# Zero products behind the narrower product of a bank, and another order of the steps

## The chip, the core and the metric

The kernel runs on one NeuronCore of a Trainium2 chip. Five engines work side by side, each through its own instructions in program order: TensorE (PE in the profile; its weight loads are the row PEld), VectorE (DVE), ScalarE (ACT), GpSimd (POOL) and SyncE (SP). They wait for one another through semaphores. The metric is the device time of one execution in microseconds, lower is better. Before the change the median of three runs is 690.34 us (690.3 to 690.51).

## The reference

Four batches of cross-covariance attention are followed by a two-layer network with a tanh GELU:

```python
B, N, C = (4, 6080, 256)
qn = q / (np.linalg.norm(q, axis=1, keepdims=True) + 1e-06)
kn = k / (np.linalg.norm(k, axis=1, keepdims=True) + 1e-06)
s = kn.transpose(0, 2, 1) @ qn / tau          # 256 x 256 per batch
a = np.exp(s - s.max(-1, keepdims=True))
a /= a.sum(-1, keepdims=True) + 1e-09
x = (v @ a).reshape(B * N, C)                 # 24320 tokens of 256
h = x @ w_in                                  # 2048 wide
g = 0.5 * h * (1.0 + np.tanh(c * (h + 0.044715 * h * h * h)))
out = g @ w_out
```

Inputs and output are float32 in DRAM; the products are made in bfloat16.

## The kernel before, in words

**Stages.** The attention matrix of a batch and `w_in` are multiplied into one matrix `aw` (256 x 2048), so that a token block needs two products: `v` with `aw`, then GELU, then `w_out`. The tokens are cut into 25 blocks, numbered 0 to 24: five of 1024 and one of 960 tokens in each of the first three batches (so blocks 5, 11 and 17 have 960), and five of 1024, one of 512 (block 23) and one of 448 (block 24) in the last. A block is worked on in two halves of tokens; half a block is 512, 480, 256 or 224 columns. While one batch's blocks are worked on, the next batch's q and k are loaded and its Gram matrix, norms and `aw` are made.

**Two recursions.** Most of both products are made by a scheme with seven products in place of eight, whose sums are formed inside the accumulator banks.

- First layer, for block n and index i, steps `m1` to `m7` (`small`, L539): `m1` starts bank RB. `wcq` (L584, on ACT) copies RB into another bank, on which `m2` then accumulates; `m6` goes on in RB. `m5` starts a bank that `wy5` (ACT, L590) copies to a buffer. `wap` (DVE, L593) writes RB plus that buffer into a further bank, on which `m3` accumulates; `m7` goes on in RB; `wax` (DVE, L596) writes RB plus the buffer into `xw`; `m4` ends RB. `wGp`, `wGs`, `wGr`, `wGx` (ACT, L602 and L604) are the four GELUs. Some columns are made by plain products instead: `g` (`plain`, L493) and its GELU `G` (L510).
- Second layer, for block n and half h of the features: `T1` to `T4` (L671 on DVE; `T3` of blocks 1 to 22 is an accumulating DMA from POOL, L665) form sums of GELU outputs; `M1` to `M7` (`product`, L675) are the products, four matmuls a step; `cq` (ACT, L739), `y5` (ACT, L742), `ap` (DVE, L745) and `ax` (DVE, L748) play the parts of the `w` steps; `c11`, `c12`, `c21`, `c22` (DVE, L718) turn results for the stores (L731; SP, in the last blocks POOL and ACT too). Block 24 uses direct products `D` (`direct`, L698).

**Banks.** All accumulators share one pool of eight banks of 512 float32 columns, which the order names by the letters a to g and z. Any step that starts an accumulator says which bank it takes. Blocks of different widths use the same banks.

**Zeros.** `wcq`, `wap`, `cq` and `ap` let ACT or DVE write a sum into a bank on which matmuls then accumulate with `start=False`. The code wants every column of that sum to have been written by a matmul since the bank was last started. `BITS` holds, for each bank, how many columns that is. When the last product that started a bank was narrower than the new sum (480 columns before one of 512, say), `fill` (L484), called by `set_sum` (L566) and `next_sum` (L693), issues a matmul of zeros over the missing columns right where the new sum begins; the copying engine's write comes after it.

```python
def fill(acc, tag, w):
    x0 = BITS.get(tag, 0) // 32 * 32
    for x in range(x0, w, 256):
        mm(acc[:, x : min(w, x + 256)], lhsT=ones_bf, rhs=zeros_bf[:, 0 : min(w, x + 256) - x],
           start=x == 0, stop=True)
    BITS[tag] = max(w, BITS.get(tag, 0))
```

**The order.** After a prologue written as code (the first batch's Gram matrix, until about 38 us), the whole program is a string, `ORDER`, of 3,946 words, each a step such as `cq@b:10` (step `cq` of block 10 into bank b) or `m6.3:17` (step `m6`, index 3, block 17). They are issued one after another (`run`, L850), so the string sets the order on every engine's queue. `lq`, `lk` and `lv` issue the loads of q, k and v on POOL and wait for the last matmul issued before them; `lt` (L446) issues the transposing load of a half of v on SP; `vs` (DVE, L534 to L537) forms sums of v for `m4` to `m7`; `row` (L205) are Gram products; `qsq`, `ksq`, `f1` to `f3`, `sp`, `sa` are the norms; `aw` and `ac` (L375, L384, L386) make `aw`; the words that begin with `p` prepare the combined `w_out`.

Of the kernel before, what the change touches and what calls it, by code (L numbers as in the profile page):

```python
# [932 lines left out]
g.0_0@e:1 g.15_1@c:0 g.1_0@a:0 G.13_0:0 g.2_0@g:1 g.12_1@f:0 lv.1:1 G.1_0:0 g.7_0@d:0 g.2_1@a:0
G.0_0:1 pS4:0 G.2_0:1 g.10_1@e:0 G.12_1:0 ksq.0:1 qsq.0:1 row.0_5@z:1 g.10_0@g:0 G.7_0:0 lk.1:1
G.10_1:0 G.15_1:0 g.14_1@f:0 g.9_1@d:0 row.0_3:1 row.0_0:1 g.11_0@e:0 G.5_0:0 G.9_1:0 G.14_1:0
G.10_0:0 row.0_4:1 lt.1:1 G.2_1:0 g.13_1@c:0 T1.1:0 g.8_0@b:1 g.10_0@d:1 g.4_0@f:1 row.0_1:1 pNA:0
G.13_1:0 G.11_0:0 f1.0:1 T1.0:0 M1.1@g:0 lv.0:2 g.3_0@a:1 G.3_0:1 g.11_1@c:0 T3.1:0 f2.0:1 pA12:0
G.11_1:0 G.8_0:1 G.4_0:1 T2.0:0 f3.0:1 m1.1@e:1 M1.0:0 lq.2:1 row.0_2:1 M5.1@a:0 vs:1 g.0_1@c:1
row.1_3:1 row.1_2:1 wcq.1@b:1 G.0_1:1 G.10_0:1 row.1_5:1 row.1_4:1 lq.3:1 row.1_0:1 g.4_1@f:1 cq@c:0
G.4_1:1 row.1_1:1 M5.0:0 g.3_1@d:1 m5.1@f:1 m6.1:1 gc:1 G.3_1:1 wy5.1:1 y5:0 T2.1:0 lk.2:1 sp.0@z:1  # L940
M2.0:0 qsq.1:1 m2.1:1 g.12_0@d:1 M2.1:0 lv.1:2 T3.0:0 wap.1@f:1 c11:0 g.8_1@a:1 G.12_0:1 wGp.1:1
ksq.1:1 m7.1:1 m3.1:1 wax.1:1 g.10_1@d:1 f1.1:1 wGs.1:1 G.10_1:1 g.7_1@g:1 m5.5@b:1 G.8_1:1 T4.0:0
m1.6@f:1 lk.3:1 M6.0:0 m4.1:1 G.7_1:1 wy5.5:1 m1.5@d:1 wGr.1:1 sa.0:1 wcq.5@a:1 M6.1:0 g.2_1@g:1
f2.1:1 m2.5:1 ap@b:0 wcq.6@e:1 f3.1:1 m6.5:1 m6.6:1 m2.6:1 wGp.5:1 M7.0:0 M7.1:0 wap.5@a:1 lt.1:2
wGx.1:1 G.2_1:1 sp.1@z:1 g.12_1@g:1 T4.1:0 lt.0:2 M3.0:0 lq.4:1 wGp.6:1 qsq.2:1 m3.5:1 m7.5:1 M3.1:0
sa.1:1 ax:0 ksq.2:1 f1.2:1 M4.1:0 m5.6@e:1 wax.5:1 c12:0 lk.4:1 f2.2:1 M4.0:0 g.11_1@b:1 f3.2:1
sp.2@z:1 c21:0 wGs.5:1 G.12_1:1 sa.2:1 wGx.5:1 wy5.6:1 g.7_0@a:1 g.15_0@g:1 g.15_1@e:1 wap.6@c:1
ksq.3:1 row.2_1@z:1 m3.6:1 row.3_1:1 m4.5:1 qsq.3:1 G.15_1:1 wGs.6:1 G.11_1:1 f1.3:1 row.3_0:1
m7.6:1 row.3_3:1 G.7_0:1 row.3_5:1 row.2_0:1 wax.6:1 g.0_0@e:2 lk.5:1 T1.0:1 g.12_0@c:2 lq.5:1
T3.0:1 f2.3:1 row.3_4:1 wGr.5:1 m4.6:1 m1.3@b:2 G.0_0:2 m1.1@a:2 g.4_0@d:2 row.2_5:1 row.2_2:1  # L950
row.2_3:1 vs:2 G.12_0:2 wcq.3@e:2 m5.1@c:2 G.15_0:1 wGr.6:1 m6.3:2 m2.3:2 T1.1:1 wcq.1@g:2 wy5.1:2
m5.3@f:2 row.2_4:1 row.3_2:1 gc:1 f3.3:1 m6.1:2 g.11_0@c:1 m2.1:2 wy5.3:2 wGp.3:2 wGp.1:2 G.4_0:2
wGx.6:1 G.11_0:1 M5.1@f:1 wap.1@e:2 M5.0:1 wap.3@g:2 m5.5@d:2 T2.0:1 m3.3:2 m7.3:2 sp.3@z:1 y5:1
wGs.3:2 wax.3:2 lv.0:3 m7.1:2 g.8_1@c:2 M1.1@f:1 wGx.3:2 lk.6:1 m4.3:2 T3.1:1 T2.1:1 g.12_1@g:2
M1.0:1 qsq.4:1 ksq.4:1 m3.1:2 G.8_1:2 wax.1:2 g.4_1@c:2 wGr.3:2 G.12_1:2 cq@b:1 G.4_1:2 f1.4:1
m1.2@g:2 wGs.1:2 T4.0:1 wcq.2@c:2 f2.4:1 M2.0:1 M6.1:1 sa.3:1 m5.2@e:2 lv.1:3 f3.4:1 M2.1:1 m2.2:2
wy5.5:2 wy5.2:2 m1.5@d:2 m6.2:2 lq.6:1 wGp.2:2 m4.1:2 wcq.5@e:2 c11:1 wGr.1:2 wap.2@c:2 wGx.1:2
lt.1:3 M6.0:1 m2.5:2 lt.0:3 c22:0 ap@f:1 wGp.5:2 m7.2:2 wax.2:2 m3.2:2 g.0_1@a:2 sp.4@z:1 m6.5:2
M3.0:1 m4.2:2 wGs.2:2 qsq.5:1 ksq.5:1 sa.4:1 wap.5@e:2 G.0_1:2 f1.5:1 M3.1:1 wGr.2:2 wGx.2:2
m1.7@c:2 m7.5:2 m3.5:2 m1.6@a:2 wGs.5:2 g.8_0@g:2 c12:1 wcq.6@f:2 f2.5:1 G.8_0:2 M7.0:1 m5.6@e:2  # L960
wax.5:2 wcq.7@g:2 m2.6:2 m4.5:2 f3.5:1 M7.1:1 m2.7:2 m6.6:2 wy5.6:2 wGr.5:2 m5.7@e:2 sp.5@z:1 T4.1:1
m6.7:2 wGp.6:2 ax:1 M4.0:1 wap.6@d:2 sa.5:1 m7.6:2 wy5.7:2 wap.7@f:2 lq.7:1 wGx.5:2 wax.6:2 qsq.6:1
wGx.6:2 row.4_1@z:1 M4.1:1 m4.6:2 row.4_3:1 m7.7:2 m3.6:2 row.5_1:1 row.5_0:1 row.5_2:1 row.5_3:1
wGp.7:2 ksq.6:1 m1.2@e:3 c21:1 wax.7:2 m4.7:2 row.4_2:1 m3.7:2 wGs.6:2 wGr.6:2 wcq.2@b:3 f1.6:1
row.5_5:1 wGr.7:2 row.4_4:1 m1.1@g:3 m2.2:3 wGs.7:2 g.0_1@d:3 wGp.2:3 wcq.1@a:3 lk.7:1 vs:3 m5.1@c:3
row.4_0:1 T1.0:2 f2.6:1 g.0_0@f:3 m5.2@b:3 m6.1:3 row.5_4:1 m6.2:3 wy5.1:3 G.0_0:3 m2.1:3 T3.0:2
wap.1@c:3 wy5.2:3 G.0_1:3 M1.0@f:2 wGp.1:3 wGx.7:2 m3.1:3 g.8_1@b:3 m7.1:3 wGs.1:3 G.8_1:3 T1.1:2
M1.1:2 wap.2@d:3 wax.1:3 cq@a:2 lv.0:4 row.4_5:1 m3.2:3 m5.3@c:3 m4.1:3 M2.1:2 m1.3@b:3 wGx.1:3
lv.1:4 wy5.3:3 wGs.2:3 f3.6:1 gc:1 T2.1:2 wcq.3@c:3 wGr.1:3 T2.0:2 m7.2:3 sp.6@z:1 T3.1:2 M2.0:2
M5.0@d:2 wax.2:3 qsq.7:1 c11:2 m6.3:3 m2.3:3 m4.2:3 M6.1:2 wGp.3:3 wGr.2:3 wap.3@g:3 c22:1 m5.4@f:3  # L970
m1.4@c:3 T4.0:2 m7.3:3 M5.1:2 wGx.2:3 wcq.4@e:3 wy5.4:3 y5:2 m2.4:3 m3.3:3 m6.4:3 M6.0:2 wGs.3:3
wax.3:3 wap.4@f:3 ap@d:2 m5.5@g:3 wGp.4:3 wGx.3:3 m7.4:3 lt.1:4 m3.4:3 m4.3:3 wy5.5:3 lt.0:4
m1.5@e:3 M7.0:2 wcq.5@g:3 wax.4:3 sa.6:1 wGs.4:3 m6.5:3 m2.5:3 wGx.4:3 ksq.7:1 wap.5@f:3 m4.4:3
M7.1:2 m3.5:3 m7.5:3 f1.7:1 wGr.4:3 wGp.5:3 m1.6@c:3 wGr.3:3 m5.6@g:3 M3.0:2 ax:2 wcq.6@b:3 wax.5:3
m2.6:3 wy5.6:3 lv.0:5 wGs.5:3 wGp.6:3 m6.6:3 m4.5:3 wGr.5:3 g.8_0@g:3 m1.7@f:3 G.8_0:3 f2.7:1 M4.0:2
T4.1:2 wap.6@b:3 lk.0:2 wcq.7@e:3 m3.6:3 m5.7@g:3 f3.7:1 m7.6:3 sp.7@z:1 T1.0:3 m6.7:3 wGx.5:3
wax.6:3 wy5.7:3 sa.7:1 wGx.6:3 m2.7:3 wap.7@g:3 M3.1:2 M4.1:2 wGs.6:3 wGp.7:3 c12:2 lq.0:2 m7.7:3
m4.6:3 wax.7:3 m3.7:3 g.0_1@b:4 wGr.6:3 wGs.7:3 m4.7:3 c21:2 vs:4 m1.1@d:4 m1.2@e:4 G.0_1:4 T1.1:3
wcq.1@c:4 row.7_5@z:1 row.6_5:1 wGr.7:3 m5.1@g:4 row.7_4:1 lv.1:5 m2.1:4 row.7_0:1 m5.2@a:4
row.6_1:1 m6.1:4 pow:1 row.6_0:1 wcq.2@b:4 wy5.1:4 wGx.7:3 m2.2:4 wy5.2:4 wap.1@f:4 kf:1 T3.1:3  # L980
T3.0:3 wGp.1:4 wGp.2:4 m6.2:4 row.7_2:1 row.7_3:1 m7.1:4 m1.3@g:4 wcq.3@a:4 wax.1:4 row.7_1:1
row.6_2:1 m3.1:4 wGs.1:4 lq.1:2 row.6_4:1 wGx.1:4 wap.2@c:4 T2.0:3 g.0_0@b:4 m4.1:4 row.6_3:1
m5.3@f:4 G.0_0:4 wy5.3:4 m6.3:4 m7.2:4 m2.3:4 m3.2:4 gc:1 M1.1@b:3 m5.4@f:4 wax.2:4 T2.1:3 m4.2:4
wGr.1:4 wGs.2:4 m1.4@d:4 wGp.3:4 wap.3@c:4 ksq.0:2 wGr.2:4 M1.0:3 wcq.4@a:4 M5.1@e:3 m2.4:4 m7.3:4
kr:1 wGx.2:4 wy5.4:4 m3.3:4 m6.4:4 M5.0:3 c22:2 wax.3:4 m4.3:4 wap.4@f:4 krp@z:1 m3.4:4 T4.1:3
wGp.4:4 wGs.3:4 m7.4:4 cq@a:3 M2.0:3 wGx.3:4 lt.1:5 m5.5@c:4 wGs.4:4 S.1:1 S.0:1 m1.5@f:4 wax.4:4
# [319 lines left out]
```

## Time and profile before

| | |
|---|---|
| Median of three runs | 690.34 us (690.3 to 690.51) |
| Profiled execution | 690.15 us |
| Its span, from the first to the last instruction | 688.0 us |
| PE busy | 662.0 us, 3,517 instructions recorded |
| ACT busy | 621.9 us |
| DVE busy | 612.6 us |
| Granted TensorE clock over the span | 0.998 |

The span is the time between the first and the last instruction; 2.15 us of the profiled execution lie outside it. A row of the timeline gives the start in microseconds from the span's start, the time it took, the engine, the line, the operation with its output and inputs, and in brackets how long the engine was idle before it and what released it. The ends of matmuls are modelled: a matmul of 512 columns is shown as 0.38 us long although the next one starts 0.216 us later, so lost time on PE is read from start to start. A few matmul records are missing from the trace; such a hole is as long as one matmul.

### The profile page before, as it was taken

The numbers are of one execution on the slowest core, as the hardware profiler recorded it, in microseconds if no ns is written. First come the engines' busy times: TensorE is split into PE (matmuls) and PEld (weight loads), VectorE is DVE, ScalarE is ACT, GpSimd is POOL, SyncE is SP. The second block draws the span as 40 slices with busy tenths as digits, with TensorE's granted clock in tenths as the row PEclk, the third lists the DMA queues.
The fourth block names the chain that finished last, engine by engine and source line by source line (L and its number), as shares of the span: only waits on it lengthen the run. The fifth ranks groups of instructions, "written<-read, shape, count | busy, mean of one in ns | idle before, by whom it ended". The sixth has DMA issues, their size and how long they took to land.

```text
span 688.0 us, 10545 instructions
## 1 busy us (share of the span) xinstructions
PE 662.0 (96%) x3517; PEld 336.1 (49%) x3579; DVE 612.6 (89%) x941; ACT 621.9 (90%) x1193; POOL 115.0 (17%) x181
## 2 busy tenths in 40 slices
...
GB/s 240 208 251 138 150 180 162 167 189 120 184 129 159 183 186 120 171 95 162 162 114 174 162 149 179 136 154 148 81 114 116 119 134 124 131 94 155 94 87 92
DMA packets 167848, 101.70 MB, mean 148 GB/s; under 512 B 149217, under 2 KB 152929, under 8 KB 167073
## 3 DMA queue, kind: packets, MB, share of 16 engines
...
q8 instruction: 28, 0.46, 0.3%
...
## 4 chain that ended last, share of the span: by engine, by line
PE 87%; ACT 7%; DVE 2%; DMA 2%; issue 1%; SPq 0%; DVEq 0%; ACTq 0%
PE rb L481 17%; PE p L481 16%; PE q L481 13%; PE r L481 11%; PE m L481 10%; PE h L481 10%; PE G L205 6%; ACT g L602 3%; PE awp L375 2%; DMA qk_f<-in_q_dram 1%; ACT q L584 1%; PE o L481 1%; ACT yw L590 1%; PE warm L269 1%; PE ss L263 1%
## 5 line engine op out<-in xcount | busy, mean ns | idle before, releaser
L481 PEld LDWEIGHTS <-wcomb 128*128 128x128 bf16 x1408 | 136.7, 98 | 146.4 <-issue 4.5
L602 ACT ACTIVATE g<-q 128x512 bf16<-128x512 f32 (+1 forms) x286 | 170.8, 621 | 5.3 <-PE q L481 4.4
L481 PEld LDWEIGHTS <-aw 128*128 128x128 bf16 x807 | 78.1, 98 | 81.9 <-issue 4.6
L593 DVE TENSOR_TENSOR q<-rb,yw 128x512 f32<-128x512 f32 (+2 forms) x150 | 102.1, 686 | 13.6 <-PE rb L481 4.1
L671 DVE TENSOR_TENSOR t<-g,t 128x2048 bf16<-128x2048 bf16 (+2 forms) x96 | 112.8, 1180 | 1.0 <-ACT g L510 0.8
L596 DVE TENSOR_TENSOR xw<-rb,yw 128x512 f32<-128x512 f32 (+2 forms) x150 | 100.9, 675 | 12.3 <-PE rb L481 7.1
L481 PE MATMUL rb<-tv,sw 128*128 128x512 bf16 (+3 forms) x307 | 106.6, 367 | 1.4 <-DVE q L593 0.8
L510 ACT ACTIVATE g<-h 128x512 bf16<-128x512 f32 (+1 forms) x164 | 97.1, 654 | 4.1 <-PE h L481 4.0
L584 ACT ACTIVATE q<-rb 128x512 f32<-128x512 f32 (+2 forms) x150 | 91.4, 618 | 8.1 <-PE q L481 3.3
L590 ACT ACTIVATE yw<-m 128x512 f32<-128x512 f32 (+2 forms) x150 | 92.7, 621 | 6.2 <-PE m L481 3.7
L602 ACT ACTIVATE g<-xw 128x512 bf16<-128x512 f32 (+1 forms) x143 | 92.7, 650 | 3.3 <-DVE xw L596 3.1
L481 PE MATMUL r<-g,wcomb 128*128 128x512 bf16 (+2 forms) x377 | 94.2, 373 | 1.2 <-ACT p L739 0.7
L481 PE MATMUL p<-t,wcomb 128*128 128x512 bf16 (+2 forms) x372 | 93.3, 373 | 0.5
L481 PE MATMUL h<-vT,aw 128*128 128x512 bf16 (+2 forms) x321 | 90.3, 377 | 1.8 <-DVE aw L415 1.1
L481 PEld LDWEIGHTS <-sw 128*128 128x128 bf16 x628 | 61.1, 98 | 62.4 <-issue 3.2
L602 ACT ACTIVATE g<-rb 128x512 bf16<-128x512 f32 (+1 forms) x143 | 87.7, 618 | 1.3 <-PE rb L481 1.2
L665 POOL DMA_DIRECT2D g<-g x44 | 39.5, 933 | 180.3 <-ACT g L602 78.2
L671 DVE TENSOR_TENSOR t<-g 128x2048 bf16<-128x2048 bf16 (+2 forms) x48 | 56.7, 1182 | 0.1
L481 PE MATMUL m<-tv,sw 128*128 128x512 bf16 (+3 forms) x156 | 56.1, 367 | 0.4 <-ACT yw L590 0.2
L481 PE MATMUL rb<-tv,aw 128*128 128x512 bf16 (+3 forms) x157 | 55.7, 367 | 0.2
L481 PE MATMUL rb<-vT,aw 128*128 128x512 bf16 (+3 forms) x157 | 55.0, 367 | 0.3
L481 PE MATMUL q<-vT,aw 128*128 128x512 bf16 (+3 forms) x153 | 54.1, 367 | 1.2 <-ACT q L584 1.2
...
## 6 DMA issues: line engine op xcount, KB each, us to landing
...
```

Source lines behind the costliest of these rows:

```text
L205: nc.tensor.matmul(G[b][:, jc, :], lhsT=qt[:np_, r, jc * 128 : jc * 128 + 128], rhs=kt[:np_, r, :], start=first and jc == 0, stop=jc == 1, ...
L263: nc.tensor.matmul(SS[1], lhsT=ones_bf, rhs=sq[:, 256:512], start=c == 0 and r == 0, stop=end)
L375: nc.tensor.matmul(ps, lhsT=ET[b][:, jc, ic * 128 : ic * 128 + 128], rhs=win_bf[:, jc, fs * 512 : fs * 512 + 512], start=jc == 0, stop=jc ...
L481: GATE[0] = nc.tensor.matmul(*a, skip_group_check=True, **kw)
L510: nc.scalar.activation(g_half(n, u // 8)[:, x, u % 8], hp[:, :hc], AF.Gelu_apprx_tanh)
L584: nc.scalar.activation(Q[n, i, 0][:, :w], RB[n, i][:, :w], AF.Copy)
L590: nc.scalar.activation(YW[n, i][:, :w], M5.pop((n, i))[:, :w], AF.Copy)
L593: nc.vector.tensor_add(Q[n, i, 1][:, :w], RB[n, i][:, :w], YW[n, i][:, :w])
L596: nc.vector.tensor_add(XW[n, i][:, :w], RB[n, i][:, :w], YW.pop((n, i))[:, :w])
L602: nc.scalar.activation(g[:, t, k0], x[:, :w], AF.Gelu_apprx_tanh)
L665: nc.gpsimd.dma_start(out=o, in_=quarter(n, 1, 1, h), accum_op=ALU.add)
L671: (nc.vector.tensor_add if add else nc.vector.tensor_sub)(o, a, b)
```

## The change

Two things change. First, a new function `pads` walks through the order before the program is built and finds each product that starts a bank with fewer columns than the next sum in that bank needs. Behind that product, `begun` issues the matmul of zeros over the missing columns at once, and notes the full width in `BITS`, so that `fill` finds nothing to do where the sum begins. Second, the words of `ORDER` are put in another sequence: the same 3,946 steps, of which 3,807 stand at another place (13 places away on average) and 790 of those that name a bank name another one. With the order before, 8 sums call for zeros (`cq` and `ap` of blocks 4 and 10, `wcq.6` of block 12, `ap` of block 16, `wcq.2` of block 18, `wap.1` of block 24); with the order after, there are 9 narrower products with zeros behind them.

```diff
+    def pads():
+        last, res = {}, {}
+        for pos, word in enumerate(ORDER.split()):
+            what, _, n = word.partition(":")
+            what, _, tag = what.partition("@")
+            name = what.partition(".")[0]
+            if tag in ("", "z"):
+                continue
+            hc = hc_of(int(n)) if name != "aw" else 512
+            w = hc if name in ("M1", "M5", "cq", "ap") or hc > 256 else 2 * hc
+            if name in ("wcq", "wap", "cq", "ap"):
+                if tag in last and last[tag][1] < w:
+                    res[last[tag][0]] = max(w, res.get(last[tag][0], 0))
+            else:
+                last[tag] = (pos, w)
+        return res
+
+    PADS, STEP = pads(), [0]
+
+    def begun(acc, tag, w):
+
+        end = PADS.get(STEP[0], w)
+        if end > w:
+            mm(acc[:, w:end], lhsT=ones_bf, rhs=zeros_bf[:, 0 : end - w], start=False, stop=True)
+        BITS[tag] = max(w, end)
...
@@ plain
-        BITS[tag] = w = hc if wide else t
+        w = hc if wide else t
...
+        begun(hp, tag, w)
@@ small
-            BITS[tag] = U * hc
...
+        if m in (1, 5):
+            begun(acc, tag, U * hc)
@@ product
-            BITS[tag] = hc
...
+        if first:
+            begun(ACC[n, acc], tag, hc)
...
-        for word in ORDER.split():
+        for STEP[0], word in enumerate(ORDER.split()):
             run(word)
...
 ORDER = """
-g.2_0@f:0 g.3_0@g:0 g.0_0@a:0 aw.2@b:0 aw.3@c:0 ac.2:0 vp.1@z:0 ac.3:0 g.6_0@d:0 aw.5@e:0 G.2_0:0
-G.3_0:0 vc.1_0:0 G.6_0:0 G.0_0:0 vc.1_1:0 aw.4@f:0 g.4_0@g:0 aw.6@b:0 ac.5:0 aw.7@c:0 ac.4:0
...
-wap.3@g:11 aw.3@c:2 m4.2:11 wGs.2:11 m7.3:11 m3.3:11 cq@b:10 ac.3:2 M2.1:10 wGx.2:11 m1.5@c:11
...
-m3.5:11 aw.5@e:2 M2.0:10 ac.7:2 m1.6@g:11 wy5.7:11 ac.5:2 wGs.5:11 wax.5:11 ap@f:10 M3.0:10
...
-c12:23 wax.3:24 m3.3:24 D.5_0:24 wGr.2:24 D.2_1@e:24 m4.3:24 wGs.3:24 D.2_0:24 m2.3:24 wGx.1:24
-wGp.3:24 D.0_1:24 wGr.3:24 wGx.3:24 wGx.2:24 c22:23 D.4_1:24 D.1_1:24 D.3_0:24 D.5_1:24 D.6_0:24
-D.7_0:24 D.7_1:24 D.3_1:24 D.6_1:24 c11:24 c21:24 sB:24 c12:24 c22:24 sA:24
+g.3_0@f:0 g.0_0@g:0 g.2_0@a:0 aw.2@b:0 aw.3@c:0 ac.2:0 ac.3:0 g.1_0@d:0 vp.1@z:0 vc.1_1:0 vc.1_0:0
+g.7_0@e:0 aw.5@b:0 ac.5:0 G.7_0:0 aw.4@c:0 G.2_0:0 g.5_0@e:0 ac.4:0 aw.7@a:0 ac.7:0 lk.0:1 g.4_0@b:0
+G.1_0:0 G.0_0:0 G.5_0:0 G.3_0:0 g.3_1@d:0 G.3_1:0 g.10_1@g:0 g.2_1@c:0 aw.6@e:0 g.9_0@a:0 g.1_1@f:0
...
+m4.4:11 wy5.1:11 ac.4:2 wGs.4:11 m1.3@a:11 M5.1@f:10 m5.2@g:11 T1.0:10 wGr.4:11 ac.0:2 wGp.1:11
...
+m4.2:11 T2.0:10 wy5.5:11 m3.3:11 cq@g:10 m1.5@b:11 m7.3:11 wGx.2:11 M2.1:10 wax.3:11 M2.0:10
...
+m4.5:11 ap@a:10 M3.1:10 wy5.6:11 M7.1:10 wGx.5:11 wGr.5:11 ac.5:2 T4.1:10 wap.6@e:11 m7.6:11 c22:9
...
+D.5_0:24 m3.3:24 m3.2:24 D.5_1:24 m4.3:24 wGs.3:24 D.0_0:24 wGs.2:24 wGx.2:24 D.1_0:24 D.2_1:24
+D.2_0:24 wGx.3:24 m4.2:24 D.0_1:24 wGr.3:24 wGr.2:24 D.7_0:24 D.6_1:24 D.3_0:24 D.6_0:24 c12:23
+D.7_1:24 D.3_1:24 c21:24 c11:24 c22:23 D.4_1:24 c12:24 sB:24 c22:24 sA:24
 """
```

More of the change, by code (lines that the diff above doesn't have):

```diff
@@ L933 @@
[L933 to L986, printed above, removed]
@@ new lines @@
+wap.5@a:2 f3.4:1 m6.6:2 ap@f:1 c22:0 wGr.2:2 wGx.2:2 m5.6@b:2 m3.5:2 lt.0:3 sp.4@z:1 ksq.5:1 m7.5:2
+m1.7@d:2 M7.1:1 wax.5:2 qsq.5:1 f1.5:1 sa.4:1 f2.5:1 lt.1:3 M3.1:1 M7.0:1 m4.5:2 wGs.5:2 wcq.7@a:2
+wy5.6:2 M3.0:1 m6.7:2 ax:1 m5.7@b:2 f3.5:1 wGr.5:2 wy5.7:2 m2.7:2 sp.5@z:1 M4.0:1 wGx.5:2 wap.6@c:2
+sa.5:1 m7.6:2 wap.7@b:2 wax.6:2 qsq.6:1 wGp.7:2 row.4_2@z:1 row.4_3:1 m3.7:2 m7.7:2 c12:1 ksq.6:1
+M4.1:1 lk.7:1 wGx.6:2 wGs.7:2 wax.7:2 m3.6:2 row.5_0:1 g.8_0@f:2 m4.6:2 wGs.6:2 row.5_3:1 wGr.6:2
@@ new lines @@
+m6.3:4 row.7_3:1 row.6_5:1 wax.1:4 m5.3@a:4 wap.2@f:4 m4.1:4 wGp.3:4 row.7_1:1 wGx.1:4 wy5.3:4
+wGr.1:4 T2.1:3 g.0_0@d:4 m3.2:4 M5.1:3 m7.2:4 gc:1 wGs.2:4 wap.3@a:4 M1.1@b:3 m1.4@f:4 wax.2:4 kr:1
+m7.3:4 G.0_0:4 m5.4@d:4 y5:3 krp@z:1 m4.2:4 T4.1:3 wGx.2:4 wcq.4@g:4 wax.3:4 wGr.2:4 M1.0:3 c22:2
+m2.4:4 m6.4:4 lt.0:5 wy5.4:4 cq@c:3 m4.3:4 wGr.3:4 S.0:1 T4.0:3 m5.5@d:4 m3.3:4 wap.4@e:4 wy5.5:4
+wGs.3:4 M2.0:3 wGp.4:4 th.0:1 M2.1:3 m1.5@d:4 m7.4:4 m3.4:4 M6.0:3 qsq.0:2 lv.0:6 c11:3 S.1:1
+wcq.5@a:4 m6.5:4 wGx.3:4 M6.1:3 m2.5:4 wax.4:4 m4.4:4 wap.5@g:4 m7.5:4 m5.7@b:4 m3.5:4 wGs.4:4
@@ new lines @@
+m3.3:6 G.4_1:6 wGs.3:6 M2.0:5 g.12_0@e:6 M2.1:5 wax.3:6 T2.1:5 wap.1@a:6 lq.3:2 wy5.2:6 m4.3:6
+wGx.3:6 c11:5 G.12_0:6 m7.1:6 wGr.3:6 m3.1:6 m1.2@f:6 g.12_1@e:6 M6.1:5 wcq.2@d:6 m6.2:6 row.1_0:2
+wax.1:6 m4.1:6 SW.1:1 wGs.1:6 c22:4 wap.2@c:6 G.12_1:6 wGx.1:6 wGr.1:6 m5.5@a:6 M6.0:5 row.1_2:2
+m1.5@e:6 m2.2:6 m7.2:6 m3.2:6 ap@b:5 wy5.5:6 wcq.5@a:6 wGp.2:6 M3.0:5 wGs.2:6 m2.5:6 wGp.5:6 T4.0:5
+wax.2:6 m6.5:6 m5.6@d:6 m1.6@c:6 wy5.6:6 m4.2:6 lk.4:2 wGr.2:6 wap.5@a:6 wcq.6@d:6 M3.1:5 m3.5:6
+row.1_4:2 m7.5:6 row.0_4:2 f2.1:2 c12:5 wGx.2:6 m2.6:6 wGs.5:6 m1.7@f:6 m6.6:6 m5.7@b:6 f3.1:2
@@ new lines @@
+wGs.1:7 T1.0:6 m2.2:7 T3.0:6 m7.1:7 m2.3:7 m6.2:7 M5.0@g:6 M5.1:6 wGp.2:7 T2.0:6 wax.1:7 wap.2@f:7
+wGp.3:7 T2.1:6 lq.5:2 lv.0:9 m4.1:7 m6.3:7 qsq.2:2 cq@e:6 wGr.1:7 wGx.1:7 y5:6 m3.2:7 m7.2:7 M2.0:6
+f1.2:2 f2.2:2 f3.2:2 sa.1:2 m5.3@b:7 wax.2:7 M2.1:6 wy5.3:7 wGs.2:7 wap.3@g:7 sp.2@z:2 m1.5@b:7
+sa.2:2 c11:6 wcq.5@f:7 M6.0:6 m3.3:7 m2.5:7 m4.2:7 m5.5@d:7 m7.3:7 wGx.2:7 wGs.3:7 wy5.5:7
+row.3_0@z:2 m5.6@g:7 m6.5:7 c22:5 M6.1:6 wGr.2:7 wax.3:7 m4.3:7 wGp.5:7 wap.5@d:7 wGx.3:7 wGr.3:7
+m3.5:7 lv.1:9 ap@c:6 m7.5:7 row.2_4:2 m1.6@f:7 wcq.6@a:7 T4.0:6 T4.1:6 wGs.5:7 wy5.6:7 qsq.3:2
```

593 lines of the change are left out of this document (310 added, 283 removed).

## The prediction

> **What bounds the kernel now.** I read the page first, then PE's waits, then the instructions on the zeros' tile, then the timeline around each of them.
>
> ```profile
> PE 662.0 (96%) x3517; PEld 336.1 (49%) x3579; DVE 612.6 (89%) x941; ACT 621.9 (90%) x1193; POOL 115.0 (17%) x181
> PE 87%; ACT 7%; DVE 2%; DMA 2%; issue 1%; SPq 0%; DVEq 0%; ACTq 0%
> ...
> 100.00:150.00 50.00, 49.74 (x263) 24.75 (x267) 48.89 (x80) 49.41 (x96) 11.69 (x17) 1.00 0.99 173
> ...
> 300.38 1.03 PE L481 MATMUL p<-t,wcomb 128*128 128x512 bf16 x4
> 301.24 0.38 PE L481 MATMUL rb<-tv,aw 128*128 128x512 bf16 x1
> ```
>
> The first row is the busy time by engine, the second the chain that ended last, the third one window (PE, PEld, DVE, ACT, POOL, then clock 1.00 and DMA). PE sets the time: 96% busy, 87% of the chain, at full clock. Four matmuls of 512 columns start in 0.86 us, 0.216 us each; one of 480 takes 480/512 of that. The number of matmuls stays, so only time in which PE stands still can be won. Here is that time as PE's waits name it, and the zeros.
>
> ```profile
> PE q L481 <- DVE q L745: 1.6, 3, 0.8
> PE q L481 <- ACT q L584: 1.2, 2, 0.7
> PE rb L481 <- DVE q L593: 0.8, 1, 0.8
> PE r L481 <- ACT p L739: 0.7, 1, 0.7
> ...
> L481 PE MATMUL q<-zeros_bf,ones_bf x6: 179/179/246, 182.9 to 669.7; 128*128 128x32 bf16 x5, 128*128 128x192 bf16 x1
> L481 PE MATMUL p<-zeros_bf,ones_bf x2: 179/179/179, 175.2 to 343.4; 128*128 128x32 bf16 x2
> ...
> 343.42 0.18 PE L481 MATMUL p<-zeros_bf,ones_bf 128*128 128x32 bf16 x1
> 343.66 0.58 ACT L739 ACTIVATE p<-r 128x512 f32<-128x512 f32 x1 [1.17 <-PE p L481]
> 344.29 1.02 PE L481 MATMUL r<-g,wcomb 128*128 128x512 bf16 x4 [0.69 <-ACT p L739]
> 350.22 0.18 PE L481 MATMUL q<-zeros_bf,ones_bf 128*128 128x32 bf16 x1
> 350.46 0.70 DVE L745 TENSOR_TENSOR q<-p,y 128x512 f32<-128x512 f32 x1 [1.01 <-PE q L481]
> 351.21 0.59 PE L481 MATMUL q<-g,wcomb 128*128 128x512 bf16 x2 [0.81 <-DVE q L745]
> 375.83 0.18 PE L481 MATMUL q<-zeros_bf,ones_bf 128*128 128x32 bf16 x1
> 376.07 0.58 ACT L584 ACTIVATE q<-rb 128x512 f32<-128x512 f32 x1 [1.32 <-PE q L481]
> 376.70 0.38 PE L481 MATMUL q<-vT,aw 128*128 128x512 bf16 x1 [0.69 <-ACT q L584]
> 669.67 0.25 PE L481 MATMUL q<-zeros_bf,ones_bf 128*128 128x192 bf16 x1
> 670.71 0.35 PE L481 MATMUL rb<-tv,sw 128*128 128x224 bf16 x2 [0.79 <-DVE q L593]
> 183.13 0.38 PE L205 MATMUL G<-k,q 128*128 128x256 bf16 x2
> 183.89 1.02 PE L481 MATMUL q<-g,wcomb 128*128 128x512 bf16 x3 [0.38 <-DVE q L745]
> 514.84 0.59 PE L375 MATMUL awp<-win_bf,eT 128*128 128x512 bf16 x2
> 515.80 0.38 PE L481 MATMUL q<-g,wcomb 128*128 128x512 bf16 x1 [0.37 <-DVE q L745]
> 524.98 0.38 PE L481 MATMUL rb<-tv,sw 128*128 128x512 bf16 x1
> 525.81 0.38 PE L481 MATMUL q<-vT,aw 128*128 128x512 bf16 x1 [0.46 <-ACT q L584]
> ```
>
> Those four waits are 4.3 us, and all seven of their cases stand behind zeros. At 343.42 PE issues them; only then may ACT copy into that bank, though it had stood idle for 1.17 us; PE's next instruction needs the copy and starts at 344.29. PE is in order, so all behind it waits too.
>
> **The zeros, step by step.** PE's loss, start to start, less what PE worked in between (0.03 us for 32 columns, 0.09 for 192): 343.42, 0.84; 350.22, 0.96; 375.83, 0.84; 669.67, 0.95. Where work stood between: 183.13 to 183.89 less two matmuls of 256 columns, 0.54; 514.84 to 515.80 less two of 512, 0.53; 524.98 to 525.81 less one, 0.61. The eighth (175.2) costs nothing, as other steps stand between it and the copy's user. Sum: **5.27 us**. [...]
>
> In the changed kernel the zeros stand right behind a product that starts the bank long before, so the copy waits for its source and its bank alone. The copying engines can use that: they were idle 1.17, 1.01 and 1.32 us before the copies quoted. Nine pads of 0.03 to 0.09 us replace eight: 0.0. A reader of the narrow product may wait one pad longer, 0.03 us. What is late next: the copy's own round trip, from the last source product to the first user. From the zeros at 350.22 it takes 0.99 us, of which the copying instruction is 0.70; I take 0.97 us from the end of PE's source work. The new order leaves 1.04 us of PE work there for `ap:10` (two matmuls of `aw.5`, then `m1.7`, `m6.6` and `m4.5`: 0.43 + 3 x 0.20), 1.04 for `ap:4`, 1.24 for `cq:10` and `ap:16`, over 2 for the other three; the sums that newly call for zeros have 1.24 and more. So I credit all 5.27; if a copy comes late by a queued instruction (0.6 us) at three tight places, 3.5 is left: bounds 3.5 to 5.27.
>
> **The order, in groups.** Distances below are sums of PE's own work between two words of an order, at the 0.216 us above and in proportion to columns.
>
> Short round trips between PE and ACT or DVE (`wcq`, `wap`, `wax`, `cq`, `ap`, `ax`): before, 15 are under 0.97 us, short by 2.06 us in all; after, 4, short by 0.42. They show where they are shortest, in block 17 (`m6.1` to `m7.1`, 0.71):
>
> ```profile
> 497.32 0.36 PE L481 MATMUL q<-vT,aw 128*128 128x480 bf16 x1
> 497.68 0.36 PE L481 MATMUL rb<-tv,sw 128*128 128x480 bf16 x1
> 497.88 0.36 PE L481 MATMUL q<-vT,sw 128*128 128x480 bf16 x1
> 498.37 0.36 PE L481 MATMUL rb<-tv,sw 128*128 128x480 bf16 x1
> ```
>
> Steps of 0.36 and 0.49 where 0.20 is due. That is a gain of up to 1.64. Against it, `wax` needs the single `xw` buffer, freed by the `wGx` before: under 1.5 us of PE work between that and `m4` in 19 cases after, 15 before. I take **-1.0**, bounds -1.64 and +0.5.
>
> The start. The order before begins `g.2_0 g.3_0 g.0_0 aw.2 aw.3 vp.1 g.6_0`; the new one puts `g.1_0` ahead of `vp.1`, 0.43 us of work in front of the first product that needs `ac.3`.
>
> ```profile
> 38.86 1.09 ACT L510 ACTIVATE g<-h 128x512 bf16<-128x512 f32 x2
> 42.03 1.08 ACT L510 ACTIVATE g<-h 128x512 bf16<-128x512 f32 x2 [2.08 <-PE h L481]
> 40.95 0.39 PE L481 MATMUL h<-vT,aw 128*128 128x512 bf16 x1
> 41.61 0.39 PE L481 MATMUL h<-vT,aw 128*128 128x512 bf16 x1 [0.27 <-DVE aw L386]
> 46.49 12.34 ACT L510 ACTIVATE g<-h 128x512 bf16<-128x512 f32 x25
> ```
>
> PE's 0.44 us hole at 40.95 is then covered. But ACT's first word is now `G.7_0`, whose product waits for `ac.3`: ACT starts at about 42.0, not 38.86, and the two GELUs that it did there come later. At 12.34/25 = 0.49 us a GELU, ACT's work in the new order, counted from 42.0, stays 0.2 to 0.5 us ahead of the product that reuses its bank until 57 us, then falls up to 0.7 us behind by 65 us (before: some 3 us ahead throughout). Price 0.8, bounds 0 and 1.2; with the 0.44, **+0.4**.
>
> The end. The last twelve direct products stand as before, but `c22:23` now stands between `c11:24` and `c12:24`, so SP issues two more stores ahead of block 24's four; `D.2_1` and `D.7_0` have their GELUs 1.3 and 2.1 us before them behind up to four others.
>
> ```profile
> 682.50 3.05 SPq L731 DMA_DIRECT2D out_dram<-ot  x4
> ```
>
> SP spends 3.05 us on four stores there, 0.76 each; two more at most 1.5, at least 0, as SP waited inside those 3.05. With the GELUs, **+0.7**, bounds 0 and 1.7.
>
> DMA queues. POOL's loads (`lv`, `lq`, `lk`) move with their gates; from `lv` to its `lt` there are at least 4.5 us after (1.7 before). The tightest summing DMA is `T3.1:2`: from the gate ahead of it, `lv.1:4`, to `M7.1:2` 8.94 us (9.16 before). The transposing loads, from `lt` to the first user: five under 8 us after (4.3, 5.8, 6.0, 6.5, 7.8, all `vs`), four before (5.7, 5.8, 7.3, 7.9). Landing times, first of `T3`, then of the transposes:
>
> ```profile
> DMA to landing us min/median/max: 4.5/6.6/9.8
> DMA to landing us min/median/max: 3.1/3.8/9.5
> ```
>
> At the medians all are covered, by the products between; **0**, bounds 0 and +9 (the first four at 8 us each; priced as a rival).
>
> Sum: -5.27 - 1.0 + 0.4 + 0.7 = -5.2 us. The profiled execution before took 690.15 us (span 688.0 and 2.15 outside it), so 685.0; the median of the runs stands 0.19 above: **685.2 us**.
>
> **Rivals.** (1) Given back: PE runs on, but ACT or DVE is the next bound in the dense stages (ACT 49.41 of 50 us in the window from 100). Then the zeros at 183, 343, 350 and 375 (3.2 us) are lost again: about 688.3. For it: the chain leaves PE for ACT in 7%. Against it: ACT's busy share counts overlapping instructions, 25 GELUs of 0.65 us in 12.34. (2) Slower: the transposing loads land late. If each takes L us, the first four `vs` (4.3, 5.8, 6.0, 6.5) hold DVE, and `m4` to `m7` behind it on PE, for 4L - 22.6 us. At L = 7.0 that is 5.4, the whole gain; from there it is slower, and at L = 7.4, with 7.0 us lost, the time is 692.2. Median 3.8 and no such wait of PE before speak against it, the maximum of 9.5 for it. (3) No change: PE makes up a stall by running faster after it; then 690.3. The row at 344.29 speaks against it: its four matmuls take 1.02 us as those at 300.38 do. [...] (4) More: no tail cost and the round trips in full: 682.8 to 683.5.
>
> **How the numbers follow.** Forecast (683.5 to 687.4) 0.62, given back 0.18, no change 0.03, slower 0.08, more 0.09. A measurement of this kernel tells about 0.2% (1.4 us) from no change. Faster: 0.62 + 0.09 + most of given back = 0.83; the same 0.09; slower 0.08. The range takes in "more" and given back up to 688.9 and leaves out 2 in 10: 682.8 to 688.9.
>
> **What would show it.** Right: each matmul of zeros directly behind a narrower product, with no PE wait over 0.3 us on L739, L745, L584 or L593; PE idle some 5 us less. Right on the order: the steps of 0.3 to 0.5 us in block 17 gone; ACT's first GELU at 42 us; the end after the last product longer by up to 1 us. Wrong: waits of the same size at those lines without zeros; DVE at L534 waiting for a DMA; a PE wait on POOL's sums.

## The result, and the profile after

The changed kernel takes 686.11 us (median of 4 runs, 685.57 to 686.14) beside 690.42 us for the kernel before on the same chip (4 runs, 690.3 to 691.23). The ratio is 0.9933, with a 95% interval of 0.9916 to 0.995: about 0.7% faster. Its profiled execution took 686.12 us, with a span of 684.3 us. Beside the experiments below the kernel before took 690.45 and 690.39 us, so medians of different comparisons are set side by side.

First the page (busy time, and the chain that ended last) and PE's waits in the changed kernel. A row of the waits gives the engine, what it was about to make, for what it waited and where that is made; then us in total, times, longest. Behind the first 480 lines the line numbers are about 30 higher than before: L584 is L613 now, L593 is L622, L739 is L769, L745 is L775.

```profile
PE 662.3 (97%) x3580; PEld 335.9 (49%) x3580; DVE 612.0 (89%) x941; ACT 622.2 (91%) x1193; POOL 115.1 (17%) x181
PE 90%; DMA 6%; issue 1%; DVE 1%; POOL 0%; ACT 0%; POOLq 0%; SPq 0%; DVEq 0%
```

```profile
PE G L205 <- ACT qk_g1a L131: 10.0, 2, 7.3
PE ss L257 <- DVE a L243: 1.3, 1, 1.3
PE G L205 <- DMA qk_g1b<-in_k_dram: 0.8, 1, 0.8
PE h L481 <- DVE aw L415: 0.7, 1, 0.7
PE p L481 <- DMA g<-g: 0.7, 1, 0.7
```

The four waits on the copies (4.3 us) are gone, and the chain leaves PE for ACT no more (0% where it was 7%). The first four rows lie in the prologue or at its end. The last row is new: one product waits for a summing DMA. The zeros are now the nine below (line, tile, count, durations in ns, first and last start), and where one stands, PE's next product starts with the usual pace:

```profile
L481 PE MATMUL rb<-zeros_bf,ones_bf x4: 179/179/179, 166.5 to 342.4; 128*128 128x32 bf16 x4
L481 PE MATMUL m<-zeros_bf,ones_bf x3: 179/179/179, 335.3 to 528.5; 128*128 128x32 bf16 x3
L481 PE MATMUL r<-zeros_bf,ones_bf x2: 179/212/246, 201.0 to 657.7; 128*128 128x32 bf16 x1, 128*128 128x192 bf16 x1
...
342.18 0.37 PE L481 MATMUL rb<-vT,aw 128*128 128x480 bf16 x1
342.39 0.18 PE L481 MATMUL rb<-zeros_bf,ones_bf 128*128 128x32 bf16 x1
342.41 0.36 PE L481 MATMUL rb<-tv,sw 128*128 128x480 bf16 x1
```

From the start of the zeros to the next product it is 0.02 us; at 343.42 of the kernel before it was 0.87 us.

The last rows of the timeline, before and after, show what went the other way:

```profile
681.75 1.12 PE L481 MATMUL o<-g,wcomb 128*128 128x224 bf16 x10
...
682.50 3.05 SPq L731 DMA_DIRECT2D out_dram<-ot  x4
```

```profile
673.78 2.08 PE L481 MATMUL o<-g,wcomb 128*128 128x224 bf16 x20
...
675.39 0.40 DVE L748 STREAM_TRANSPOSE ot<-c 128x256 f32<-128x256 f32 x1
...
675.82 3.56 SPq L761 DMA_DIRECT2D out_dram<-ot  x6
...
676.08 1.16 POOL L761 DMA_DIRECT2D out_dram<-ot  x2 [5.46 <-DVE ot L748]
```

PE's last product ends (as modelled) at 682.87 before and at 675.86 after, 7.0 us sooner. From there to the end of the span it is 5.2 us before (688.03) and 8.5 us after (684.35). So PE won 7.0 us, and 3.3 us of it were given back behind the last product. The prologue has no part in the gain. The first product of block 0 that the trace shows starts at 38.08 after and at 38.42 before, but `g.2`, `g.3` and `g.0` are six products, and before only five are on record: the first is missing there, as in every trace here but the changed kernel's. The second starts at 38.48 after and at 38.42 before. From the second product to the start of the last of all it is 637.12 us, where it was 644.19: 7.07 us less. All stretches below are counted from that second product.

The views leave out closing instructions. In the trace's own records POOL's last stores, and the instruction among them, are these (start, end, engine, instruction), first before, then after:

```
before  678.62 679.20 GpSimd DMA_DIRECT2D out_dram<-ot
before  679.06 686.14 GpSimd DRAIN
before  679.19 679.78 GpSimd DMA_DIRECT2D out_dram<-ot
after   676.08 676.67 GpSimd DMA_DIRECT2D out_dram<-ot
after   676.52 683.56 GpSimd DRAIN
after   676.66 677.24 GpSimd DMA_DIRECT2D out_dram<-ot
```

A closing DRAIN of 7.08 us before and 7.04 after begins with POOL's last stores, and in both traces the span ends only behind it (the DRAIN at 686.14 and the span at 688.03 before, at 683.56 and 684.35 after). Before, SP had done its last wait for a store by 687.25, a microsecond after the end of POOL's DRAIN: the DRAIN was hidden. After, SP is done at 681.18 and everything waits for POOL until 683.56: 2.4 us. The rest of the 3.3 us is SP's own: from the start of PE's last product to the end of SP's waits it is 4.6 us before and 5.6 after, 0.9 more.

### The profile page after: what moved, and what is told of

It is laid out like the page before. It is cut to its first block, busy times and chain, and to the rows that moved or that the text cites. A ratio compares the mean times of both kernels' runs of the same rounds, so it can differ in the third digit from the quotient of the medians.

```text
span 684.3 us, 10611 instructions
## 1 busy us (share of the span) xinstructions
PE 662.3 (97%) x3580; PEld 335.9 (49%) x3580; DVE 612.0 (89%) x941; ACT 622.2 (91%) x1193; POOL 115.1 (17%) x181
## 4 chain that ended last, share of the span: by engine, by line
PE 90%; DMA 6%; issue 1%; DVE 1%; POOL 0%; ACT 0%; POOLq 0%; SPq 0%; DVEq 0%
PE rb L481 18%; PE p L481 17%; PE q L481 15%; PE r L481 11%; PE h L481 10%; PE m L481 10%; PE G L205 5%; DMA qk_g1b<-in_k_dram 2%; PE awp L375 2%; DMA qk_g1a<-in_q_dram 1%; DMA g<-g 1%; PE o L481 1%; DMA out_dram<-ot 1%; PE ss L186 0%; PE ss L263 0%
## 5 line engine op out<-in xcount | busy, mean ns | idle before, releaser
L631 ACT ACTIVATE g<-q 128x512 bf16<-128x512 f32 (+1 forms) x286 | 168.8, 622 | 5.6 <-PE q L481 5.1
L622 DVE TENSOR_TENSOR q<-rb,yw 128x512 f32<-128x512 f32 (+2 forms) x150 | 102.4, 686 | 14.5 <-PE rb L481 4.6
L481 PE MATMUL rb<-tv,sw 128*128 128x512 bf16 (+3 forms) x314 | 109.0, 367 | 0.1
L481 PE MATMUL p<-t,wcomb 128*128 128x512 bf16 (+2 forms) x384 | 95.9, 373 | 0.0
L481 PE MATMUL h<-vT,aw 128*128 128x512 bf16 (+2 forms) x336 | 93.5, 377 | 0.8 <-DVE aw L415 0.7
L613 ACT ACTIVATE q<-rb 128x512 f32<-128x512 f32 (+2 forms) x150 | 90.1, 611 | 4.4 <-PE rb L481 2.7
L481 PE MATMUL q<-vT,sw 128*128 128x512 bf16 (+3 forms) x157 | 56.0, 367 | 0.0
L481 PE MATMUL q<-vT,aw 128*128 128x512 bf16 (+3 forms) x157 | 55.8, 367 | 0.0
```

Of the source, the lines that this page charges most:

```text
L481: GATE[0] = nc.tensor.matmul(*a, skip_group_check=True, **kw)
L613: nc.scalar.activation(Q[n, i, 0][:, :w], RB[n, i][:, :w], AF.Copy)
L622: nc.vector.tensor_add(Q[n, i, 1][:, :w], RB[n, i][:, :w], YW[n, i][:, :w])
L631: nc.scalar.activation(g[:, t, k0], x[:, :w], AF.Gelu_apprx_tanh)
```

## The experiments

My theory after the first comparison had three parts. The zeros cost their round trip where the sum begins (5.3 us by starts in the old order). The new order lets PE gain a little beside that, but loses 3.3 us at the end through one word, `c22:23`, whose last two stores POOL issues late. And the one wait of PE on a summing DMA costs 0.8 us. The rivals: that the order itself, not the place of the zeros, made the gain; and that the longer end comes from SP's stores, not from POOL.

**The two parts of the change apart.** The first kernel has the order before and the new place of the zeros; the second has the order after and the old `fill` alone.

```diff
+    PADS, STEP = pads(), [0]
...
+        if m in (1, 5):
+            begun(acc, tag, U * hc)
```

> The order of before with the zeros placed behind the narrower products: the first part of the change alone. Theory (each zero product that stands where the sum begins costs PE the copy's round trip, 0.84 us by ACT and 0.96 us by DVE, less the PE work written between the sum's word and its first user, 5.29 us over the eight): the last matmul starts 5.3 us earlier than before, near 677.3, the end stays 5.4 us behind it, and the time is 685.1 (685.0 to 686.2). PE's waits on L739, L745, L584 and L593 vanish. Rival (the copies were late by their own queues too, so the next wait takes their place): under 3.5 us are won, 687 or more. Rival (only the new order lets the copy start earlier): no gain, 690.3.

Measured: 684.62 us (median of 6, 683.52 to 688.01), ratio 0.9895, interval 0.9844 to 0.9946. That is 5.8 us under the 690.45 us of the kernel before beside it, and 0.4 under the range that I expected. The median is 1.5 us below the changed kernel's too, though the two intervals overlap.

The rows show where more than the counted 5.27 us came from. Matched product by product with the kernel before, PE gains at the seven places of the prediction, and 0.35 us more at each of two others, 377.69 and 526.81 of the kernel before. Some 6.2 us are won in all, if a stall of this profiled execution is left out (it stands in the last section). Here is the first of the two places, before and in this kernel:

```profile
376.07 0.58 ACT L584 ACTIVATE q<-rb 128x512 f32<-128x512 f32 x1 [1.32 <-PE q L481]
377.04 0.60 ACT L590 ACTIVATE yw<-m 128x512 f32<-128x512 f32 x1
377.13 0.38 PE L481 MATMUL rb<-tv,sw 128*128 128x512 bf16 x1
377.69 0.59 PE L481 MATMUL h<-vT,aw 128*128 128x512 bf16 x2 [0.18 <-ACT yw L590]
```

```profile
378.02 0.38 PE L481 MATMUL rb<-tv,sw 128*128 128x512 bf16 x1
378.23 0.60 PE L481 MATMUL h<-vT,aw 128*128 128x512 bf16 x2
```

The zeros at 375.83 hold up not only the copy that needs them, but ACT's whole queue: its later copy `yw` came late too, and PE waited for that as well (0.56 us from start to start, where 0.21 is due).

```diff
 ORDER = """
-g.2_0@f:0 g.3_0@g:0 g.0_0@a:0 aw.2@b:0 aw.3@c:0 ac.2:0 vp.1@z:0 ac.3:0 g.6_0@d:0 aw.5@e:0 G.2_0:0
...
+g.3_0@f:0 g.0_0@g:0 g.2_0@a:0 aw.2@b:0 aw.3@c:0 ac.2:0 ac.3:0 g.1_0@d:0 vp.1@z:0 vc.1_1:0 vc.1_0:0
```

> The order of after with the zeros back where each sum begins: the second part of the change alone. By the same theory the nine zero products cost, sum by sum, 0 (cq of block 4), 0.41, 0.84, 0.44, 0.96, 0 (wcq.1 of block 12), 0.56, 0.41 and 0.96: 4.6 us more than after, so 690.7 (689.9 to 691.2) and the last matmul at 680.2. The new order alone is then worth nothing against before, as what it wins on PE it loses behind the last matmul. Rival (the order itself hides the zeros): 687 or less.

Measured: 690.97 us (11 runs, 690.43 to 691.26), ratio 0.9996, interval 0.9974 to 1.0018. PE's waits in this kernel:

```profile
PE q L481 <- DVE q L745: 1.2, 2, 0.8
PE rb L481 <- DVE q L593: 1.0, 2, 0.8
PE p L481 <- DMA g<-g: 0.7, 1, 0.7
PE q L481 <- ACT q L584: 0.7, 2, 0.5
PE rb L481 <- ACT q L584: 0.7, 1, 0.7
PE r L481 <- ACT p L739: 0.3, 1, 0.3
```

With the old `fill` the waits on the copies come back, at other places, 3.9 us of them; from the second product of block 0 to the last it is 642.18 us, 5.06 more than with both parts, and by the medians 4.86 more. So by the medians the whole gain is the place of the zeros: 5.8 us in the old order, 4.9 in the new one. The rival that the order made it is out: as changed, the new order alone is worth nothing that can be told from no change, since what it wins on PE (2.0 us) it loses again behind the last product.

**The one word at the end.** In the third kernel `c22:23` stands directly behind `c12:23` again, all else as in the changed kernel. The fourth is the opposite: the kernel before, with `c22:23` moved as late as the change has it.

```diff
-D.2_0:24 wGx.3:24 m4.2:24 D.0_1:24 wGr.3:24 wGr.2:24 D.7_0:24 D.6_1:24 D.3_0:24 D.6_0:24 c12:23
-D.7_1:24 D.3_1:24 c21:24 c11:24 c22:23 D.4_1:24 c12:24 sB:24 c22:24 sA:24
+D.2_0:24 wGx.3:24 m4.2:24 D.0_1:24 wGr.3:24 wGr.2:24 D.7_0:24 D.6_1:24 D.3_0:24 D.6_0:24 c12:23 c22:23
+D.7_1:24 D.3_1:24 c21:24 c11:24 D.4_1:24 c12:24 sB:24 c22:24 sA:24
```

> After, with one word moved: c22:23 stands directly behind c12:23, so block 23's last stores are issued some 4 us before the last matmul and not behind it. Theory (POOL's closing DRAIN ends about 7.0 us after the last store that POOL issues, 676.5 to 683.6 in after, and the program's end waits for it): the drain ends before SP's own waits, the end comes 2.4 us earlier by the drain and up to 0.9 us by SP's shorter list, and the time is 682.8 to 683.8. Rival (two more stores on SP set the late end): 685.2. Rival (the landing of block 24's stores sets it): 686.1.

```diff
-wGp.3:24 D.0_1:24 wGr.3:24 wGx.3:24 wGx.2:24 c22:23 D.4_1:24 D.1_1:24 D.3_0:24 D.5_1:24 D.6_0:24
-D.7_0:24 D.7_1:24 D.3_1:24 D.6_1:24 c11:24 c21:24 sB:24 c12:24 c22:24 sA:24
+wGp.3:24 D.0_1:24 wGr.3:24 wGx.3:24 wGx.2:24 D.4_1:24 D.1_1:24 D.3_0:24 D.5_1:24 D.6_0:24
+D.7_0:24 D.7_1:24 D.3_1:24 D.6_1:24 c11:24 c21:24 c22:23 sB:24 c12:24 c22:24 sA:24
```

> Before, with the same word moved the other way: c22:23 stands behind block 24's first two turns, as late as in after. Theory of the drain: POOL's last store is issued 0.8 to 1.1 us after the last matmul starts, the drain ends 7.0 us later, near 690.6, and the time is 690.3 + 3.3 = 693.6 (692.8 to 694.2). Rival (SP's list): 691.2. Rival (no effect): 690.3.

Measured: the third takes 682.71 us (4 runs, 682.3 to 683.42), ratio 0.9875 (0.9824 to 0.9925), 3.4 us under the changed kernel; the fourth 693.67 us (11 runs, 693.58 to 695.65), ratio 1.004 (1.0015 to 1.0064), 3.2 us over the kernel before. In the timeline of the third the word's transposition and POOL's stores stand five microseconds earlier, and in the fourth they stand behind the last products:

```profile
670.11 0.40 DVE L748 STREAM_TRANSPOSE ot<-c 128x256 f32<-128x256 f32 x1
...
670.81 1.16 POOL L761 DMA_DIRECT2D out_dram<-ot  x2 [0.44 <-DVE ot L748]
```

```profile
682.42 0.40 DVE L718 STREAM_TRANSPOSE ot<-c 128x256 f32<-128x256 f32 x1
...
683.11 1.16 POOL L731 DMA_DIRECT2D out_dram<-ot  x2 [5.10 <-DVE ot L718]
```

From the start of the last product to the end of the span it is 5.36 us in the third and 8.78 in the fourth (8.75 in the changed kernel, 5.41 before). POOL's DRAIN runs from 671.25 to 678.29 and from 683.56 to 690.63. One word, moved in either order, carries the whole longer end.

**POOL's drain or SP's stores.** The fifth kernel leaves `c22:23` late, but ScalarE issues block 23's stores that POOL issued. The edit is wider than its expectation says: it moves four stores, the two late ones of the second half and also the two of the first half, which POOL issues at 669.36 in the changed kernel.

```diff
-            store(n, tj, (nc.sync,) * 4 if n != LAST - 1 else (nc.sync, nc.sync, nc.gpsimd, nc.gpsimd))
+            store(n, tj, (nc.sync,) * 4 if n != LAST - 1 else (nc.sync, nc.sync, nc.scalar, nc.scalar))
```

> The changed kernel, with the two stores of block 23's second half that GpSimd issues given to ScalarE instead; the word c22:23 stays where the change put it. Theory A (the end waits for GpSimd's closing drain, which runs some 7.05 us after its last store is issued): without late stores GpSimd drains early, the last matmul starts at about 675.6 us as before, the span from there on falls from 8.75 to about 6.4 us, and the time is 686.1 - 2.4 = 683.7 us. Theory B (the end is long because c22:23's sum, transposition and stores themselves come late): the span behind the last matmul stays at 8 us or more, 685.5 to 686.5 us.

Measured: 685.66 us (7 runs, 685.26 to 686.26), ratio 0.991 (0.9878 to 0.9942). The total lies in theory B's range, but the span behind the last product doesn't: from the start of the last product to the end it is 6.63 us, 2.1 less than with POOL's stores and near theory A's 6.4. The total hides it because PE lost nearly as much as the end won: in the profiled execution the last product starts 2.25 us later, of which 0.36 is a later end of the prologue and 1.89 PE's loss. The trace names the cause. ACT's own queue (first) and PE (second), in the fifth kernel:

```profile
667.16 0.53 ACT L633 ACTIVATE g<-q 128x448 bf16<-128x448 f32 x1
669.55 0.86 ACTq L761 DMA_DIRECT2D out_dram<-ot  x2
670.46 0.54 ACT L633 ACTIVATE g<-rb 128x448 bf16<-128x448 f32 x1 [2.77 <-DVE xw L625]
```

```profile
668.87 0.55 PE L481 MATMUL rb<-tv,sw 128*128 128x224 bf16 x4
671.05 1.31 PE L481 MATMUL o<-g,wcomb 128*128 128x224 bf16 x12 [1.63 <-ACT g L633]
```

In the changed kernel that GELU runs at 667.31. Here the two stores of the first half stand ahead of it on ACT and wait for DVE; the GELU comes 3.15 us later (some 0.5 of it because this execution is that late by then), and PE waits 1.63 us for it. So with POOL's stores gone 2.1 of the 3.3 us go; by the trace of the changed kernel the DRAIN stands bare for 2.4. The other 0.9 to 1.2 us stay with POOL out of it. They go with the late stores themselves, which SP issues ahead of block 24's; no run takes these away alone. For this smaller part the rival, that SP's stores make the longer end, fits the trace.

**The summing DMA.** In the changed kernel `M7.1:2` waits for `T3.1:2`. In the sixth kernel `T3.1:2` is issued ahead of `lv.1:4`; on POOL's queue the load issued at 121.77 in the changed kernel then stands behind it, while the one at 120.70 stays ahead. The seventh has this edit and that of the third kernel.

```diff
-lv.1:4 wy5.3:3 wGr.1:3 wGs.2:3 wcq.3@c:3 wax.2:3 M5.0:2 m2.3:3 sp.6@z:1 cq@a:2 T2.1:2 m5.4@f:3
+T3.1:2 lv.1:4 wy5.3:3 wGr.1:3 wGs.2:3 wcq.3@c:3 wax.2:3 M5.0:2 m2.3:3 sp.6@z:1 cq@a:2 T2.1:2 m5.4@f:3
...
-ksq.7:1 T3.1:2 lv.0:5 c11:2 M6.0:2 m1.5@f:3 m3.3:3 wcq.4@b:3 T4.0:2 m2.4:3 wGx.2:3 wax.3:3 wcq.5@e:3
+ksq.7:1 lv.0:5 c11:2 M6.0:2 m1.5@f:3 m3.3:3 wcq.4@b:3 T4.0:2 m2.4:3 wGx.2:3 wax.3:3 wcq.5@e:3
```

> The changed kernel, with the summing transfer T3.1:2 issued ahead of the vb loads of lv.1:4 on GpSimd's queue. Theory A (it lands late because two loads stand ahead of it): TensorE's 0.66 us wait at 130 us on a DMA goes, the last matmul starts near 674.8 us, time 685.3 us. Theory B (the time of the landing is set by the other transfers under way, or the gate lv.1:4 is itself late next): the wait stays or moves to a matmul that uses vb, 686.1 us, up to 0.5 us more.

> The changed kernel with both edits: c22:23 directly behind c12:23, and T3.1:2 ahead of lv.1:4. If the two are independent: 682.7 (the first alone) - 0.8 = 681.9 us, the last matmul at about 674.5 us and 5.4 us behind it. If the second is worth nothing: 682.7 us.

Measured: 685.15 us (7 runs, 685.06 to 685.52), ratio 0.9905 (0.987 to 0.994), 0.96 us under the changed kernel; with both edits 681.99 us (6 runs, 681.77 to 682.17), ratio 0.9856 (0.982 to 0.9892). The issue of the summing DMA on POOL and the product that needs it, first in the changed kernel, then in the sixth:

```profile
120.70 0.53 POOL L441 DMA_DIRECT2D vb<-in_v_dram  x1 [2.41 <-PE rb L481]
121.77 0.50 POOL L441 DMA_DIRECT2D vb<-in_v_dram  x1 [0.54 <-PE rb L481]
122.33 0.92 POOL L694 DMA_DIRECT2D g<-g  x1
...
130.09 0.38 PE L481 MATMUL m<-tv,sw 128*128 128x512 bf16 x1
131.14 1.02 PE L481 MATMUL p<-g,wcomb 128*128 128x512 bf16 x4 [0.66 <-DMA g<-g]
```

```profile
121.16 0.90 POOL L694 DMA_DIRECT2D g<-g  x1
121.75 0.84 POOL L441 DMA_DIRECT2D vb<-in_v_dram  x1
...
130.00 0.38 PE L481 MATMUL m<-tv,sw 128*128 128x512 bf16 x1
130.21 1.03 PE L481 MATMUL p<-g,wcomb 128*128 128x512 bf16 x4
```

The sum is issued 1.17 us earlier and lands at 129.08 instead of 131.09; PE goes on after 0.21 us instead of 1.05. Theory A holds, for the one load that changed its place. The two edits add up (682.71 - 0.83 = 681.88, measured 681.99): this kernel beats both others, by 8.4 us over the one before.

**ACT's first GELUs.** The eighth kernel lets ACT begin its GELUs as early as before the change.

```diff
-g.3_0@f:0 g.0_0@g:0 g.2_0@a:0 aw.2@b:0 aw.3@c:0 ac.2:0 ac.3:0 g.1_0@d:0 vp.1@z:0 vc.1_1:0 vc.1_0:0
+g.3_0@f:0 g.0_0@g:0 g.2_0@a:0 G.3_0:0 G.0_0:0 G.2_0:0 aw.2@b:0 aw.3@c:0 ac.2:0 ac.3:0 g.1_0@d:0 vp.1@z:0 vc.1_1:0 vc.1_0:0
```

> The changed kernel with the first three GELUs (G.3_0:0, G.0_0:0, G.2_0:0) issued ahead of the addition aw.2@b:0, so that ScalarE begins them near 38.9 us instead of 42.1. The prediction's term for the start says that the later start costs 0.8 us: the time falls to 685.3 us. What the trace of the changed kernel shows (TensorE busy 20.00 of 20 us between 40 and 60) says that nothing waits for them: 686.1 us, within 0.3 us; and the 0.14 us gap ahead of the first products of block 0 may come back as 0.4 us.

Measured: 685.54 us (7 runs, 684.97 to 687.42), ratio 0.9912 (0.9879 to 0.9945). The median is 0.57 us under the changed kernel, between the two expectations. ACT in the changed kernel, then in the eighth:

```profile
42.09 5.00 ACT L539 ACTIVATE g<-h 128x512 bf16<-128x512 f32 x10 [3.18 <-PE h L481]
```

```profile
38.76 1.57 ACT L539 ACTIVATE g<-h 128x512 bf16<-128x512 f32 x3
41.93 1.08 ACT L539 ACTIVATE g<-h 128x512 bf16<-128x512 f32 x2 [1.59 <-PE h L481]
```

ACT does start 3.3 us earlier, and PE makes nothing of it: from the second product of block 0 to one and the same product near 58 us it is 19.63 us here and 19.66 in the sixth kernel, whose start is that of the changed one; to one near 68 us the difference is still 0.03. What the profiled execution of the eighth won lies elsewhere: its prologue ended 0.17 us earlier, and PE's wait for the summing DMA at 130 us was 0.3 us (0.66 in the changed kernel's). Neither is known to come from the GELUs.

## Why the prediction was right, and where it was not

Forecast 685.2 us, measured 686.11, inside the likeliest case's own range (683.5 to 687.4). The near hit is the sum of errors of both signs. Against the forecast, PE gained 1.20 us more (7.07, not 5.87), the prologue of the profiled execution was 0.06 longer and the time outside the span 0.38 shorter, the median stood 0.20 lower against the profiled execution, and the end cost 2.64 more (3.34, not 0.7): +0.92 in all. That a loss at the end and a gain on PE nearly made up for each other was luck.

- **The zeros, -5.27: right in mechanism, too small.** With this part alone the time fell by 5.8 us in the old order, and without it the new order is 4.9 slower. The count took PE's loss at the sums alone. It left out that ACT, held up at the sum, is late with its later copies too. In the old order that is two waits of 0.35 us, and some 6.2 us were won by the rows of the first experiment, beyond the upper bound of 5.27. By the same count (a round trip of 0.84 or 0.96 us less PE's work up to the first user) the new order's nine would have cost 4.57, and 5.06 was measured on PE. None of the three tight places I named lost it again.
- **The end, +0.7 with bounds 0 and 1.7: this step failed.** It measured +3.34. I had seen that `c22:23` moved late and counted SP's issue of its two stores there and the late GELUs. The word's other two stores are POOL's, and I did not count them: POOL's drain of 7.05 us was covered by SP's waits by 1.1 us before, and stood bare by 2.4 us after (2.1 by the fifth kernel). The rest, 0.9, is within my bounds. The end of POOL's program appears in no row that I read; a cost that a profile keeps hidden by a microsecond was the one to bound.
- **The start, +0.4: wrong in size, by the +0.8 in it.** The hole of 0.44 us was covered as forecast, with 0.14 us left (41.31 in the timeline), so about -0.3. ACT started at 42.09, as forecast, but PE stood still nowhere in the stretch where I had ACT fall behind (window, PE, PEld, DVE, ACT, POOL, clock). As modelled ends can hide a short wait in such a row: from start to start too, no step between 41.7 and 131.1 us is over 0.30. The eighth kernel shows that the early GELUs are worth 0.0:

```profile
60.00:80.00 20.00, 20.00 (x113) 10.28 (x112) 19.22 (x30) 18.49 (x34) 3.72 (x7) 1.00 0.86 142
```

  My count of ACT's work, at 0.49 us a GELU, put ACT up to 0.7 us behind, and PE shows nothing of it.
- **Short round trips, -1.0 (bounds -1.64 and +0.5).** The steps of 0.36 and 0.49 us in block 17 are gone. With the old `fill`, the order made PE 2.01 us quicker from the second to the last product (642.18, not 644.19). Of that some 1.1 is the smaller loss at its own zeros (5.06, not 6.2) and 0.3 the start; it lost 0.8 at the summing DMA, so some 1.4 are left for the round trips, within my bounds. That is worked out and not isolated by a run.
- **DMA queues, 0.** I named `T3.1:2` as the tightest sum, with 8.94 us. It took 8.76 us to land and was issued late behind two loads, and PE lost 0.83 us: one of the signs that I listed as wrong did show. I had judged it by the median of 6.6, with a maximum of 9.8 beside it, and counted its 8.94 us from the gate ahead of it, not from its issue.
- **The rivals.** Given back (688.3) did not occur on PE: no wait on ACT or DVE took the place of the old ones. Late transposing loads (692.2) did not occur either; DVE's sums of v wait for PE only, as the row on their line shows, with us and times:

```profile
  PE rb L481: 2.2, 5
```

  No change (690.3) is out, since the stalls were not made up: behind the changed kernel's wait of 0.66 us, which ends at 131.14, PE's next four products of 512 columns take 0.86 us to the one at 132.00, 0.215 each, as the four at 300.38 did in the kernel before. More (682.8 to 683.5, without a cost at the end) is nearly what the kernel without the late word takes, 682.71.
